# An attention block feeding a two-layer network: one attention stop on TensorE per chunk instead of two, and a new layout of the PSUM banks

## The chip, the cores and the metric

The kernel runs on one core of one Trainium2 chip. The metric is device microseconds of one execution, the median of several runs: 623.57 us for the kernel before (three runs, 623.25 to 624.53).

## The reference

Inputs are q, k and v of 4 batches, 8 heads, 768 positions and 64 features, and two weight matrices of 512 x 2048 and 2048 x 512. All numbers are float32. Each query sees the keys less than 16 positions away, and beside them 24 summary keys: the maximum over each block of 32 keys, whose values are the block's mean. The output of attention becomes 3072 rows of 512 numbers and goes through two layers with a squared ReLU between them.

```python
scores_l = scale * np.matmul(q, k.transpose(0, 1, 3, 2))
mask_l = np.abs(pos[:, None] - pos[None, :]) < window
scores_s = scale * np.einsum('bhsd,bhnd->bhsn', q, k_sum) + np.log(block)
a = np.exp(scores_all - np.max(scores_all, axis=-1, keepdims=True))
a = a / (np.sum(a, axis=-1, keepdims=True) + 1e-09)
attn = np.matmul(a, v_all)
h = np.maximum(x @ w_in, 0.0)
out = h * h @ w_out
```

## The kernel before

A *tile* is 128 positions of one batch with all 8 heads: 24 tiles, numbered 0 to 23, six to a batch. A *chunk* is two tiles, 256 rows of x: 12 chunks. The hidden width of 2048 is cut into 16 *f tiles* of 128.

**The two layers.** To keep float32 accuracy with the faster matmul format, x, the weights and the squares are each split in a high and a low part. `ffn1` (L380) does the first layer of one f tile for one chunk: 12 matmuls of 256 columns into half a PSUM bank. `squares` (L413) makes r = relu on ScalarE, the high part gh of r squared on ScalarE, the full square in PSUM on VectorE and the low part gl on VectorE. `ffn2` (L419) adds 6 matmuls of 512 columns for that f tile into the chunk's two output banks. When the 16th f tile is in, `evict` (L432) copies the outputs out of PSUM and stores them.

**The attention of a tile.** `scores_by_group` (L262) computes the scores of a tile: 32 small matmuls (64 in the trace, since a float32 matmul is two instructions) on array tiles of 64 x 32. `softmax` (L310) takes each head: VectorE scales, masks and takes the maximum (L300), ScalarE takes the exponential and its sum (L308). `inverse` and `norm` divide by the sum, norm on GpSimd. `turn` (L333) transposes the probabilities in 12 blocks on VectorE into pT. `outputs` (L348) multiplies them with the values: 16 matmuls (32 in the trace) on array tiles of 128 x 64 into the bank x_ps. `split_x` (L373) makes the high part xh on ScalarE and the low part xl on VectorE; these are the input of `ffn1`.

**The order of the work** is written out by hand, and each engine runs its part of it in that order. The first part, `START` (L43), is a list of tokens for tiles 0 to 5 and chunks 0 and 1 (F1 is ffn1, T is a transpose on TensorE, O outputs, S scores, PK place_k, KT and VT the reductions over key and value blocks, XH and XL the parts of split_x). The rest is a loop over chunks 2 to 11 in *slots* of two f tiles (L460): first layer of both, then second layer of the two f tiles before (`finish`), then the squares of this slot with the attention steps that belong to it, and at the end of the slot the steps in `last`, among them scores and outputs. `steps` (L474) gives each tile twelve steps, two to a slot; in chunk c the tiles 2c+2 to 2c+4 are at different steps (L622 to L624). So chunk c stops the two layers on TensorE twice: at the end of slot f = 2 for outputs of tile 2c+2 and scores of 2c+3, and at the end of slot f = 10 for outputs of 2c+3 and scores of 2c+4. Chunk 2 differs a little: there the scores of tile 7 and the outputs of tile 6 stand alone.

**PSUM** has eight banks: two for the scores of one tile (s_ps), one for x_ps, three that rotate for ffn1's results and for transposes (ph), two for the outputs (o_ps).

**Loads** go through SyncE's queue (SP): q, k and v of a tile two tiles ahead into buffers that two tiles share in turn, and for the next batch k and v transposed (kv) in four pieces, from which `sum_k` and `sum_v` (L174, L179) make the summary keys and values; `place_k` and `place_v` copy these beside a tile's own keys and values.

Of the kernel before, what the change touches and what calls it, by code (L numbers as in the profile page):

```python
# [73 lines left out]
def attn_ffn_kernel(ctx: ExitStack, tc: tile.TileContext, q, k, k0, kt, v, vt, v0, w, masks, gmasks, ident, mean, out):  # L74
# [7 lines left out]
    ps_x = ctx.enter_context(tc.tile_pool(name="ps_x", bufs=1, space=bass.MemoryType.PSUM))  # L82
    ps_h = ctx.enter_context(tc.tile_pool(name="ps_h", bufs=3, space=bass.MemoryType.PSUM))
# [26 lines left out]
    vsum = const.tile([P, NPAIR, 32], F32, name="vsum")  # L110

# [137 lines left out]
    def scores(g, p0, p1):  # L249


        if g not in s_ps:
            s_ps[g] = ps_s.tile([P, 2, NPAIR, P], F32, name="s_ps")
        for p in range(p0, p1):
            for r, s in ((0, 0), (1, 1), (0, 1), (1, 0)):
                rs, ss = slice(r * 64, r * 64 + 64), slice(s * 64, s * 64 + 64)
                nc.tensor.matmul(  # L257
                    s_ps[g][ss, r, p, 0:NK], lhsT=q_sb[g % 2][rs, s, p, :], rhs=by_run(g)[rs, :, s, p, :],
# [3 lines left out]
    def scores_by_group(g):  # L262

        s_ps[g] = ps_s.tile([P, 2, NPAIR, P], F32, name="s_ps")
        for p in range(NPAIR):
            for r, i in ((0, 0), (1, 2), (0, 1), (1, 3), (0, 2), (1, 0), (0, 3), (1, 1)):
                s, u = divmod(i, 2)  # L270
                rs = slice(r * 64, r * 64 + 64)
                nc.tensor.matmul(  # L272
                    s_ps[g][i * GQ : i * GQ + GQ, r, p, 0:GK], lhsT=q_sb[g % 2][rs, s, p, u * GQ : u * GQ + GQ],
                    rhs=by_pair(g)[rs, s, p, u * GQ : u * GQ + GK], start=True, stop=True,
                )

    def scores_kt(g, p0, p1):

        if g not in s_ps:
            s_ps[g] = ps_s.tile([P, 2, NPAIR, P], F32, name="s_ps")  # L280
        for p in range(p0, p1):
            for k0, k1 in ((0, 96), (96, NK)):
                for r, s in ((0, 0), (1, 1), (0, 1), (1, 0)):
# [4 lines left out]
                        s_ps[g][ss, r, p, k0:k1], lhsT=q_sb[g % 2][rs, s, p, :], rhs=keys, start=True, stop=True  # L288
                    )

    def mask_max(g, h):
# [5 lines left out]
        if half not in nmx:  # L297
# [3 lines left out]
            out=e_sb[:, h, 0:n], in0=s_ps[g][:, h % 2, h // 2, 0:n], in1=m, scale=-scale, scalar=3.0e38,  # L301
# [24 lines left out]
    def turn_pe(g, half):  # L326

        tp = ps_h.tile([P, 4, P], F32, name="ph")
# [19 lines left out]
    def outputs(g):  # L348
        x_ps[g] = xp = ps_x.tile([P, NPAIR, P], F32, name="x_ps")
# [30 lines left out]
    def ffn1(c, f):  # L380
        ph = ps_h.tile([P, 4, P], F32, name="ph").rearrange("p a b -> p (a b)")[:, 0:CT]
# [78 lines left out]
    def slot(c, f, side, last):  # L460
# [4 lines left out]
        for i in range(2):  # L465
            for do in side[i]:
                do()
# [3 lines left out]
        for do in last:  # L471
            do()
# [237 lines left out]
```

## Time and profile before

| | |
|---|---|
| median of three runs | 623.57 us (623.25 to 624.53) |
| the profiled execution | 624.3 us, its span 622.5 us |
| TensorE matmul busy | 597.6 us, 96% |
| VectorE busy | 404.8 us, 65% |
| ScalarE busy | 291.6 us, 47% |
| GpSimd busy | 89.7 us, 14% |
| mean granted TensorE clock | 0.992 |

PE is TensorE's matmuls, PEld its weight loads, DVE is VectorE, ACT is ScalarE, POOL is GpSimd and SP is SyncE, whose queue issues the transfers. A matmul's end is modelled and matmuls overlap, so a busy TensorE can still be slowed. A row of a group or of the timeline names the line of the kernel, the engine, the operation, the tile written and those read, the shape, and how many there are; in a timeline the first two numbers are start and length in us, and brackets tell how long the engine had been idle and what released it. The chain of waits follows the work that ended last, back from the end; its pieces also begin with start and length.

### The profile page before, as it was taken

The numbers are of one execution on the slowest core, as the hardware profiler recorded it, in microseconds if no ns is written. First come the engines' busy times: TensorE is split into PE (matmuls) and PEld (weight loads), VectorE is DVE, ScalarE is ACT, GpSimd is POOL, SyncE is SP. The second block draws the span as 40 slices with busy tenths as digits, with TensorE's granted clock in tenths as the row PEclk, the third lists the DMA queues.
The fourth block names the chain that finished last, engine by engine and source line by source line (L and its number), as shares of the span: only waits on it lengthen the run. The fifth ranks groups of instructions, "written<-read, shape, count | busy, mean of one in ns | idle before, by whom it ended". The sixth has DMA issues, their size and how long they took to land.

```text
span 622.5 us, 14548 instructions
## 1 busy us (share of the span) xinstructions
PE 597.6 (96%) x5792; PEld 535.7 (86%) x5792; DVE 404.8 (65%) x1237; ACT 291.6 (47%) x850; POOL 89.7 (14%) x83
## 2 busy tenths in 40 slices
PE   1699999999999999999999999999999999999997
PEld 1488888988989988998989989899889989889996
DVE  4889989767756757757558668566566566563222
ACT  2779887333444353443534444434525524433322
POOL 2555762001100000000100000001100000000000
PEclk9979999999999999999999999999999999999999
DMA  8999610464042341320331422411302300000000
GB/s 296 381 346 330 210 73 18 154 199 107 26 120 70 85 120 41 113 70 34 69 94 61 120 67 87 119 52 45 78 20 49 104 1 26 35 1 2 35 1 34
DMA packets 55107, 60.58 MB, mean 97 GB/s; under 512 B 40320, under 2 KB 40448, under 8 KB 52992
## 3 DMA queue, kind: packets, MB, share of 16 engines
q1 hardware_dynamic: 55040, 59.67, 31.7%
q8 instruction: 45, 0.74, 0.5%
q14 instruction: 22, 0.18, 0.1%
HBM read 53.36 MB, written 6.29 MB: 96 GB/s over the span
## 4 chain that ended last, share of the span: by engine, by line
PE 91%; DMA 3%; DVE 2%; ACT 2%; SPq 1%; issue 0%; POOL 0%; DVEq 0%; POOLq 0%
PE ph L385 42%; PE o_ps L426 41%; PE x_ps L354 4%; PE s_ps L272 2%; DMA w_raw<-in_w 2%; DMA q_sb<-in_q 2%; PE ph L330 1%; PE s_ps L287 0%; ACT e_sb L308 0%; DVE w_sb L243 0%; ACT w_sb L117 0%; PE s_ps L257 0%; SPq L167 0%; DVE sm L317 0%; SPq L121 0%
## 5 line engine op out<-in xcount | busy, mean ns | idle before, releaser
L385 PE MATMUL ph<-xh,w_sb 128*128 128x256 f32 x1536 | 272.5, 280 | 0.2 <-DVE gl L410 0.2
L385 PEld LDWEIGHTS ph<-xh,w_sb 128*128 128x128 f32 x1536 | 238.2, 189 | 9.2 <-DVE gl L410 0.4
L426 PE MATMUL o_ps<-w_sb,gh 128*128 128x512 f32 x768 | 238.0, 391 | 0.0
L385 PE MATMUL ph<-xl,w_sb 128*128 128x256 f32 x768 | 213.3, 278 | 0.3 <-DVE xl L371 0.3
L426 PEld LDWEIGHTS o_ps<-w_sb,gh 128*128 128x128 f32 x768 | 137.1, 188 | 24.9 <-issue 0.2
L426 PE MATMUL o_ps<-w_sb,gl 128*128 128x512 f32 x384 | 151.4, 394 | 0.9 <-DVE gl L410 0.9
L406 DVE TENSOR_TENSOR ph<-ph,r 128x256 f32<-128x256 f32 x192 | 82.5, 430 | 103.8 <-ACT r L394 101.4
L394 ACT ACTIVATE r<-ph 128x256 f32<-128x256 f32 x180 | 68.4, 380 | 170.9 <-PE ph L385 170.2
L385 PEld LDWEIGHTS ph<-xl,w_sb 128*128 128x128 f32 x768 | 144.9, 189 | 0.5 <-DVE xl L371 0.5
L308 ACT ACTIVATE e_sb<-e_sb,nmx 128x88 f32<-128x88 f32 (+1 forms) x192 | 70.1, 367 | 66.2 <-DVE nmx L300 66.2
L410 DVE TENSOR_TENSOR gl<-ph,gh 128x256 fp32r<-128x256 f32 x192 | 81.5, 425 | 23.7 <-PE ph L385 0.5
L341 DVE STREAM_TRANSPOSE pT<-e_sb 32x256 f32<-32x256 f32 x216 | 94.1, 436 | 3.4
L324 POOL TENSOR_TENSOR e_sb<-e_sb,sm 128x352 f32<-128x352 f32 (+1 forms) x43 | 35.8, 833 | 409.3 <-DVE nmx L300 355.2
L426 PEld LDWEIGHTS o_ps<-w_sb,gl 128*128 128x128 f32 x384 | 72.2, 188 | 15.7 <-DVE gl L410 1.3
L401 ACT ACTIVATE gh<-r 128x256 fp32r<-128x256 f32 x192 | 80.4, 419 | 11.4 <-DVE r L396 5.4
L371 DVE TENSOR_TENSOR xl<-x_ps,xh 128x512 fp32r<-128x512 f32 x24 | 16.6, 690 | 48.8 <-ACT xh L368 48.8
L368 ACT CAST xh<-x_ps 128x512 fp32r<-128x512 f32 x24 | 14.0, 583 | 54.0 <-PE x_ps L354 53.6
L236 POOL TENSOR_TENSOR w_raw<-w_raw 128x1024 int32<-128x1024 int32 x16 | 35.3, 2213 | 24.2 <-DVE w_raw L232 8.3
L354 PEld LDWEIGHTS x_ps<-pT,v_sb 128*64 128x64 f32 x768 | 25.4, 141 | 13.4 <-issue 11.4
L308 ACT ACTIVATION_READ_ACCUMULATOR e_sb<-e_sb,nmx 128x1 f32 x192 | 36.1, 188 | 0.0
L354 PE MATMUL x_ps<-pT,v_sb 128*64 128x64 f32 x768 | 29.0, 229 | 5.4 <-issue 4.1
L300 DVE CUSTOM_DVE_ANT_0 e_sb<-s_ps,gmask_sb 128x88 f32<-128x88 f32 x144 | 27.8, 240 | 0.1
(50 smaller groups left out, 297.3 us busy)
## 6 DMA issues: line engine op xcount, KB each, us to landing
w_raw<-in_w SPq DMA_DIRECT2D x16, 1024.0 KB, 14.1
v_sb<-in_v SPq DMA_DIRECT2D x24, 384.0 KB, 3.9
kv<-in_kt SPq DMA_DIRECT2D x16, 384.0 KB, 4.5
q_sb<-in_q SPq DMA_DIRECT2D x24, 256.0 KB, 4.6
out<-ob SPq DMA_DIRECT2D x24, 256.0 KB, 2.0
k_sb<-in_k SPq DMA_DIRECT2D x18, 256.0 KB, 5.0
kv<-in_vt SPq DMA_DIRECT2D x12, 384.0 KB, 3.8
k_sb<-in_k SPq DMA_DIRECT2D x18, 128.0 KB, 4.9
```

Of the source, the lines that this page charges most:

```text
L236: nc.gpsimd.tensor_tensor(out=hi, in0=hi, in1=lo, op=ALU.add)
L300: nc.vector.tensor_tensor_reduce(out=e_sb[:, h, 0:n], in0=s_ps[g][:, h % 2, h // 2, 0:n], in1=m, scale=-scale, scalar=3.0e38, op0=ALU.add, ...
L308: nc.scalar.activation(e, e, AF.Exp, bias=nmx[half][:, i : i + 1], scale=-1.0, accum_out=sm[half][:, i : i + 1])
L324: eng.tensor_mul(out=e, in0=e, in1=sm[half].unsqueeze(2).to_broadcast([P, 4, n]))
L341: nc.vector.transpose(out=pT[g % 2][j * 32 : j * 32 + 32, :, i * 32 : i * 32 + 32], in_=e_sb[i * 32 : i * 32 + 32, :, c : c + 32],)
L354: nc.tensor.matmul(xp[o : o + 64, h // 2, s * 64 : s * 64 + 64], lhsT=v_sb[g % 2][:, s, h * 64 : h * 64 + 64], rhs=pT[g % 2][:, h, s * 64 ...
L385: nc.tensor.matmul(ph, lhsT=w_sb[f][:, w, cc * P : (cc + 1) * P], rhs=x[c][:, cc, :], start=(n == 0), stop=(n == 3 * NC4 - 1))
L394: nc.scalar.activation(r, ph, AF.Relu)
L401: nc.scalar.activation(gh, r, AF.Square)
L406: nc.vector.tensor_mul(out=ph, in0=ph, in1=r)
L410: nc.vector.tensor_sub(out=gl, in0=ph, in1=gh.bitcast(F32))
L426: nc.tensor.matmul(o_ps[c][tt], lhsT=g_[:, ts_], rhs=w_sb[f][:, w, DM:], start=(first and n == 0), stop=(last and n == 2),)
```

## The change

Three things change together.

1. **The attention of a chunk is dealt anew.** `period(a)` replaces `steps(g)`: it holds the steps of tiles a and a+1 in eight slots, the first tile in the first four, the second in the last four. The two outputs stand together at the end of the eighth, and right behind them the scores of both next tiles, `scores_by_group` now doing two tiles at a time; then the four parts of split_x, and the loads of two tiles each. In chunk c the eighth slot of the period is f = 12. In the start, the scores of tile 7 come with those of tile 6, with the loads of its q and k and its place_k ahead of them.
2. **The banks are six fixed tiles.** Banks 0 and 1 take the scores of even tiles, 2 and 3 those of odd ones. Banks 4 and 5 are the first layer's, by turns from slot to slot, and take the outputs of an odd and an even tile. In the start, first-layer results and transposes take banks 3 to 5 from a list in order of release.
3. **Two f tiles share a bank,** one in each half, and `squares` works on both at once, 512 columns wide: one relu, one high square, one product, one difference where there were two of each.

```diff
@@ START, its end
-MU24 L:kw1 F1.25 GL24v L:v5 F1.26 RE25v MU25 SQ25 GL25v F2.23 XH4a RE26v MU26 XL4v F2.24 SQ26 GL26v KT1 F1.27
+MU24 L:kw1 F1.25 GL24v L:v5 L:k7 L:q7 F1.26 RE25v MU25 SQ25 GL25v F2.23 XH4a RE26v MU26 XL4v F2.24 SQ26 GL26v KT1 F1.27
-KT0 O5 PK6 VT0 S6.0 XH5a XL5v
+KT0 O5 PK6 VT0 PK7 XH5a S6.0 XL5v
@@ banks
-    ps_x = ctx.enter_context(tc.tile_pool(name="ps_x", bufs=1, space=bass.MemoryType.PSUM))
-    ps_h = ctx.enter_context(tc.tile_pool(name="ps_h", bufs=3, space=bass.MemoryType.PSUM))
+    r_sb = const.tile([P, 2, CT], F32, name="r")
+    gh_sb = const.tile([P, 4, CT], F32R, name="gh")
+    gl_sb = const.tile([P, 4, CT], F32R, name="gl")
+    bank = [ps_s.tile([P, DM], F32, name=n, tag=f"{n}{i}") for i, n in enumerate(["s_ps"] * 4 + ["ph"] * 2)]
@@ scores_by_group
+        for t in (g, g + 1):
+            s_ps[t] = [bank[t % 2 * 2 + r].rearrange("a (p k) -> a p k", p=NPAIR) for r in range(2)]
...
@@ outputs
-        x_ps[g] = xp = ps_x.tile([P, NPAIR, P], F32, name="x_ps")
+        xp = bank[2 if g < FROM_GROUPS - 1 else 5 if g < FROM_GROUPS else 5 - g % 2]
@@ squares
-    def squares(ph):
-        r = relu(ph, nc.scalar)
-        gh = high_square(r)
+    def squares(ph, k):
+        r = relu(ph, r_sb.rearrange("p a b -> p (a b)"), nc.scalar)
+        gh, gl = (b[:, 2 * k : 2 * k + 2, :].rearrange("p a b -> p (a b)") for b in (gh_sb, gl_sb))
+        high_square(gh, r)
         square(ph, r)
-        return gh, low_square(ph, gh)
+        low_square(gl, ph, gh)
+        return [(gh_sb[:, 2 * k + i, :], gl_sb[:, 2 * k + i, :]) for i in range(2)]
@@ slot
-        ph = [ffn1(c, f + i) for i in range(2)]
+        ph = bank[4 + f // 2 % 2]
+        for i in range(2):
+            ffn1(c, f + i, ph[:, i * CT : (i + 1) * CT])
         done = finish()
+        for do in before:
+            do()
+        for i, g_ in enumerate(squares(ph, f // 2 % 2)):
+            behind.append((c, f + i, *g_, f + i == 0, f + i == NF - 1))
...
+        for do in after:
+            do()
         for do in last:
             do()
@@ steps replaced by period
+    def period(a):
+        before, after, last = [[] for _ in range(8)], [[] for _ in range(8)], [[] for _ in range(8)]
+        b, t = divmod(a, NT)
+        if a >= n_g:
+            return before, after, last
+        if b and t == 0:
+            after[1] += [lambda: place_v(a), lambda: place_v(a + 1)]
+        after[0].append(lambda: softmax(a, 0, 3))
+        before[1].append(lambda: softmax(a, 3, 6))
+        after[1] += [lambda: softmax(a, 6, 8), lambda: inverse(0), lambda: norm(a, 0, nc.gpsimd)]
+        before[2] += [lambda: inverse(1), lambda: norm(a, 1, nc.gpsimd)]
+        after[2].append(lambda: turn(a, 0, 3))
+        before[3].append(lambda: turn(a, 3, 8))
+        after[3].append(lambda: turn(a, 8, 12))
+        before[4].append(lambda: softmax(a + 1, 0, 4))
+        after[4].append(lambda: softmax(a + 1, 4, 6))
+        before[5] += [lambda: softmax(a + 1, 6, 8), lambda: inverse(0), lambda: norm(a + 1, 0, nc.gpsimd)]
+        before[5] += [lambda: inverse(1), lambda: norm(a + 1, 1, nc.gpsimd)]
+        before[6].append(lambda: turn(a + 1, 0, 5))
+        after[6].append(lambda: turn(a + 1, 5, 8))
+        before[7].append(lambda: turn(a + 1, 8, 12))
+        if b + 1 < B and t:
+            for n, p in enumerate(((0, 1), (2, 3))[t // 4]):
+                last[3 * n].append(lambda p=p: load_kv(b + 1, p))
+                after[3 * n + 2].append(lambda p=p: sum_k(b + 1, p))
+                after[3 * n + 2].append(lambda p=p: sum_v(b + 1, p))
+        if b + 1 < B and t == 4:
+            after[6] += [lambda: place_k(a + 2), lambda: place_k(a + 3)]
+        last[7] += [lambda: outputs(a), lambda: outputs(a + 1)]
+        if a + 2 < n_g:
+            last[7].append(lambda: scores_by_group(a + 2))
+        last[7] += [lambda: split_x(a), lambda: split_x(a + 1)]
+        if a + 2 < n_g:
+            last[7] += [lambda g=g: load_v(g) for g in (a + 2, a + 3)]
+        if a + 4 < n_g:
+            last[7] += [lambda g=g: load_qk(g) for g in (a + 4, a + 5)]
+        return before, after, last
@@ the start's banks
+    free, held = [3, 4, 5], {}
...
         elif op == "F1":
-            ph_of[i] = ffn1(*units[i][:2])
+            held["F1", i] = free.pop(0)
+            ph_of[i] = ffn1(*units[i][:2], bank[held["F1", i]][:, 0:CT])
...
         elif op == "GL":
+            free.append(held.pop(("F1", i)))
@@ the loop
+        softmax(6, 0, 3)
...
             for f in range(0, NF, 2):
-                side, last = [[], []], []
-                at(side, last, 2 * c + 2, f + (4 if c == 2 else 6))
-                at(side, last, 2 * c + 3, f - 2)
-                at(side, last, 2 * c + 4, f - 10)
-                slot(c, f, side, last)
+                n = (f + 2) // 2 % 8
+                slot(c, f, *(w[n] for w in period(2 * c + (2 if n else 4))))
```

More of the change, by code (lines that the diff above doesn't have):

```diff
@@ L252, in scores @@
         if g not in s_ps:
-            s_ps[g] = ps_s.tile([P, 2, NPAIR, P], F32, name="s_ps")
+            s_ps[g] = [bank[r].rearrange("a (p k) -> a p k", p=NPAIR) for r in range(2)]
         for p in range(p0, p1):
@@ L389, in ffn1, with relu @@
         return ph
-    def relu(ph, eng):
-        r = work.tile([P, CT], F32, name="r", tag="r")
+    def relu(ph, r, eng):
         if eng is nc.scalar:
@@ L397, in relu, with high_square @@
         return r
[L399 to L400 removed]
+    def high_square(gh, r):
         nc.scalar.activation(gh, r, AF.Square)
```

92 lines of the change are left out of this document (26 added, 66 removed).

## The prediction

> **What bounds the kernel now.** I read the page first, then the chain of waits in order of time, then the timeline of TensorE around single attention blocks.
>
> ```profile
> span 622.5 us, 14548 instructions
> PE 597.6 (96%) x5792; PEld 535.7 (86%) x5792; DVE 404.8 (65%) x1237; ACT 291.6 (47%) x850; POOL 89.7 (14%) x83
> PE 91%; DMA 3%; DVE 2%; ACT 2%; SPq 1%; issue 0%; POOL 0%; DVEq 0%; POOLq 0%
> ```
>
> TensorE carries 91% of the chain. What matters is whether it ever waits after the written-out start. The chain shows one period of the steady part (start us, us, what):
>
> ```profile
> 198.07 1.08 PE x_ps L354 x32
> 199.15 0.89 PE s_ps L272 x60
> 200.04 2.94 PE ph L385 x24
> 202.98 2.75 PE o_ps L426 x12
> ...
> 208.47 2.75 PE o_ps L426 x12
> ...
> 213.96 2.75 PE o_ps L426 x12
> ...
> 219.46 2.75 PE o_ps L426 x12
> 222.21 1.08 PE x_ps L354 x32
> 223.29 0.89 PE s_ps L272 x60
> 224.17 1.91 PE ph L385 x15
> ```
>
> A plain slot (two f tiles) is 202.98 to 208.47, and three of them take 219.46 - 202.98 = 16.48, so 5.49 us each. From 200.04 to 224.17 are 24.13 us: four slots (21.97) and one attention block of one tile's outputs and another's scores, 2.16. There is no other engine in this chain, so a steady stretch costs exactly what TensorE's instructions and their changes of kind cost. Blocks with only outputs or only scores stand here:
>
> ```profile
> 141.22 2.80 PE o_ps L426 x12
> ...
> 146.76 2.75 PE o_ps L426 x12
> ...
> 153.42 2.76 PE o_ps L426 x12
> ...
> 160.20 2.75 PE o_ps L426 x12
> ```
>
> ```profile
> 557.32 2.75 PE o_ps L426 x12
> ...
> 564.09 2.75 PE o_ps L426 x12
> ```
>
> Less a slot of 5.49, scores of tile 7 alone cost 153.42 - 146.76 - 5.49 = 1.17, outputs of tile 6 alone 160.20 - 153.42 - 5.49 = 1.29, outputs of tile 23 alone 564.09 - 557.32 - 5.49 = 1.28.
>
> **What a block consists of.** The timeline of TensorE across one block:
>
> ```profile
> 197.68 0.40 PE L426 MATMUL o_ps<-w_sb,gl 128*128 128x512 f32 x1
> 198.00 1.15 PE L354 MATMUL x_ps<-pT,v_sb 128*64 128x64 f32 x32
> 199.08 0.96 PE L272 MATMUL s_ps<-k_sb,q_sb 64*32 64x88 f32 x64
> 199.97 0.50 PE L385 MATMUL ph<-xh,w_sb 128*128 128x256 f32 x2
> ```
>
> A 512-column matmul normally makes room for the next after 2.75/12 = 0.23 us, so outputs could begin at 197.91 and begin at 198.00: 0.09 lost. The 32 output instructions span 1.15 with their last one's own length; the form's mean is 0.22, so their starts span 0.93, while the scores begin only 1.08 after the first: 0.15 for the change of array shape where a pitch of 0.03 would do. The scores occupy 0.89 to the next first-layer matmul:
>
> ```profile
> 199.08:199.41 0.33, 0.33 (x32) 1.00 0.00 0
> 199.41:199.81 0.40, 0.40 (x56) 1.00 0.00 0
> ```
>
> These are two windows of the score matmuls alone: the first 32 begin within 0.33, the rest by 199.80, so 0.73 of starts and 0.16 of change back. The first-layer run then lasts 2.94 where others last 2.75. So of 2.16 about 0.93 + 0.74 are streaming and 0.49 are changes of kind.
>
> **The change, part by part.** Scores are issued for tiles 6 to 23, outputs likewise. Before: after scores of 6 in the start there are scores of 7 alone, outputs of 6 alone, 16 joint blocks, outputs of 23 alone. After: scores of 7 join those of 6, then 8 blocks of two outputs and two scores, then outputs of 22 and 23 together. Matmul counts, shapes and array tiles stay; only 10 of 19 interruptions go.
>
> *Second outputs in a block.* The trace has no two output sets in a row. Lower bound 0.93 (starts of one set), upper 1.08 (as before a change). I take 0.94: both sets use the same 128*64 tiles, so there is no change between them.
>
> *Second scores.* Lower bound twice the first half, 0.66; upper the whole block, 0.89. I take the middle, 0.77, since the second half above ran slower than the first. [...]
>
> *Sum in the steady part.* Before: 16 × 2.16 + 1.29 + 1.28 + 1.17 = 38.30. After: 8 × (2.16 + 0.94 + 0.77) = 30.96, and 1.28 + 0.94 = 2.22.
>
> *The end of the start.* The second place_k (PK7) now stands on VectorE ahead of the low half of x of tile 5, and scores of 7 stand on TensorE ahead of chunk 2:
>
> ```profile
> 136.38 0.26 DVE L187 COPY k_sb<-ksum 128x192 f32<-128x192 f32 x1
> 136.56 0.94 DVE L180 TENSOR_REDUCE vsum<-kv 128x24 f32<-128x768 f32 x1
> 136.72 0.96 PE L272 MATMUL s_ps<-k_sb,q_sb 64*32 64x88 f32 x64
> ...
> 137.53 0.18 DVE L183 TENSOR_SCALAR vsum<-vsum 128x24 f32<-128x24 f32 x1
> 137.61 0.50 PE L385 MATMUL ph<-xh,w_sb 128*128 128x256 f32 x2
> 137.62 0.68 DVE L371 TENSOR_TENSOR xl<-x_ps,xh 128x512 fp32r<-128x512 f32 x1
> ...
> 138.36 0.39 PE L385 MATMUL ph<-xl,w_sb 128*128 128x256 f32 x1 [0.25 <-DVE xl L371]
> ```
>
> Queued behind PK7 are only the low half and the softmax of 6. PK7 would run 137.62 to 137.88, scores of 7 from about 137.95, chunk 2 from 137.95 + 0.89 = 138.84; by then xl (0.25 later, at 138.55) is there. Before, chunk 2's first run began at 137.61 but its third matmul started only at 138.36. The whole stall shows in the chain above: the second-layer work begins at 141.22, where a first-layer run of 2.94 would have ended at 137.61 + 0.07 + 2.94 = 140.62 (the chain's pieces begin 0.07 after the timeline's, 200.04 against 199.97). So the old stall was 0.60, and the new cost is 138.84 - 137.61 - 0.60 = 0.63. Bounds: 0.25, where scores of 7 fit wholly into the stall and only PK7 shows, and 1.17, their price elsewhere. The loads of k and q for tile 7 move before the last kv load on SP; their buffers were free since the scores of 5, so nothing waits behind them.
>
> *Wide squares.* Per slot two relu, two squares, two products, two differences become one each of 512 columns. These rows price them:
>
> ```profile
> L406 DVE TENSOR_TENSOR ph<-ph,r 128x256 f32<-128x256 f32 x192 | 82.5, 430 | 103.8 <-ACT r L394 101.4
> L410 DVE TENSOR_TENSOR gl<-ph,gh 128x256 fp32r<-128x256 f32 x192 | 81.5, 425 | 23.7 <-PE ph L385 0.5
> L341 DVE STREAM_TRANSPOSE pT<-e_sb 32x256 f32<-32x256 f32 x216 | 94.1, 436 | 3.4
> L371 DVE TENSOR_TENSOR xl<-x_ps,xh 128x512 fp32r<-128x512 f32 x24 | 16.6, 690 | 48.8 <-ACT xh L368 48.8
> L368 ACT CAST xh<-x_ps 128x512 fp32r<-128x512 f32 x24 | 14.0, 583 | 54.0 <-PE x_ps L354 53.6
> ```
>
> A 512-wide operation takes 0.69 on VectorE and 0.58 on ScalarE, so a slot saves 2 × (0.43 + 0.425) - 2 × 0.69 = 0.33 on VectorE. It is worth nothing in the sum, since TensorE does not wait for it. It does make the chain longer: 0.58 + 2 × 0.69 and hand-overs, an estimated 2.4 us from the slot's last first-layer matmul, where the second-layer work of the slot before (2.75) and the next slot's first layer (2.75) cover 5.5. At the very end only 2.75 cover it, still enough; without cover it would cost at most 2.4 once.
>
> *New bank hand-overs.* Outputs of the even tile take bank 5, which the first layer of the next slot needs. This row belongs to the block shown above:
>
> ```profile
> 199.20 0.58 ACT L368 CAST xh<-x_ps 128x512 fp32r<-128x512 f32 x1 [3.01 <-PE x_ps L354]
> ```
>
> xh starts 0.27 after the last output matmul (198.00 + 0.93), so outputs to the end of xl take 0.93 + 0.27 + 0.58 + 0.69 and a hand-over, 2.5; the next first layer comes 1.08 + 0.94 + 0.77 + 0.89 = 3.68 after the outputs begin: 1.2 to spare. Outputs of the odd tile take bank 4, which the slot's own squares must leave: 2.4 against 2.75 + 1.08 = 3.8, 1.4 to spare. Both at nothing.
>
> *Total.* 38.30 - 30.96 - 2.22 - 0.63 = 4.5 us. The profiled execution took 624.3 (span 622.5 and 1.8 around it), so that run would be 619.8. It lies 0.7 above the median of the three runs, 623.57; against the median I forecast 619.1. Bounds of the unknown costs together: gain 38.30 - (8 × 4.13 + 2.36 + 1.17) = 1.7 at the least, 38.30 - (8 × 3.75 + 2.21 + 0.25) = 5.8 at the most, so 617.8 to 621.9.
>
> **The rivals.**
>
> *The blocks do not shrink.* If a second set pays as much as a set with its change (1.08 and 0.89), only entries and returns are saved and the gain is 1.7 to 2.3: 621.6. For it: no row shows two sets in a row. Against it: 0.15 and 0.16 lie plainly at the changes of shape, and within a set starts are 0.03 apart or less.
>
> *VectorE falls behind and TensorE waits: slower.* VectorE's work is dealt anew over the eight slots of a chunk. The heaviest are the one that turns the first three blocks (three transposes, the squares, and in two chunks of a batch both reductions with their scaling: 3 × 0.436 + 1.38 + 2 × 0.94 + 0.18 = 4.8) and the next (nine transposes and the squares, 3.9 + 1.4 = 5.3), of 5.49. The place where it decides is bank 5: the low half of x of the even tile stands in VectorE's queue behind four transposes and the squares, and the first layer waits for it. It turns the result when this low half is more than 1.2 + 4.5/8 = 1.8 us late in every chunk; at 2.5 us late the cost is 8 × 1.3 = 10.4, time 619.1 + 10.4 = 629.5. Against it: over a chunk VectorE needs 31 of 48 us (twice the 16.71 busy of one old period, the fourth column below, less 8 × 0.33), and lateness from the fourth slot has lighter slots behind it to run down in.
>
> ```profile
> 218.90:243.00 24.10, 24.10 (x242) 21.66 (x242) 16.71 (x54) 10.95 (x36) 1.55 (x2) 1.00 0.31 89
> ```
>
> *The start loses what the blocks gain.* Banks in the start come now from a list in order of release; five first-layer tiles and one transposed tile get another predecessor's bank than by rotation. If each came one VectorE operation later, it would be 6 × 0.43 = 2.6: 621.7. Against it: the list gives the bank that was released first, so most of them can only come earlier.
>
> **How the numbers follow.** Forecast 0.70; blocks that don't shrink 0.14; VectorE behind 0.07; the start loses 0.09. The measurement can't tell less than 0.2% (1.25 us) from no change, so faster means under 622.3: all of the forecast, most of the first and third rival (0.16 of 0.23), 0.86 with rounding; same 0.07; slower 0.07. The range 617.4 to 622.0 covers the bounds of the forecast and most of both mild rivals, and leaves out the slow one and a surplus below.
>
> **What would show it.** In the changed kernel's chain: 9 interruptions after the start where 19 were, quads of about 3.9 us (period 8 × 5.49 + 3.87 = 47.8), no other engine between them. The outputs' group should show 64 in a row with starts spanning 1.9, scores 128 in about 1.5. In the steady part TensorE should have no wait for xl, gl or pT; VectorE's busy time should fall by 10 × 8 × 0.33 = 26 us. It would be wrong if idle time of the first layer after xl appears once a chunk, or if a quad costs 4.3.

## The result, and the profile after

The changed kernel took 633.95 us (median of four runs, 631.23 to 634.45), the kernel before 623.43 in the same comparison: a ratio of 1.016, 95% interval 1.012 to 1.019. It is slower by 10.5 us. The forecast was 619.1 with a range of 617.4 to 622.0. The profiled execution took 633.53, its span 631.7 against 622.5 before, so 9.2 us are to be found. Three executions in the comparisons below took 858, 1198 and 2082 us, far above all others of their kernels, and no figure rests on them.

These are rows of the page of the changed kernel:

```profile
span 631.7 us, 14142 instructions
PE 601.6 (95%) x5792; PEld 545.1 (86%) x5792; DVE 385.4 (61%) x1077; ACT 262.5 (42%) x690; POOL 88.8 (14%) x83
PEclk9879999999999999999999998999999999999999
q8 instruction: 45, 0.74, 0.5%
PE 91%; DMA 4%; DVE 2%; issue 1%; SPq 1%; ACT 0%; DVEq 0%
```

VectorE and ScalarE have less to do, as meant (19.4 and 29.1 us less), and TensorE with the same 5792 matmuls is busy 4.0 us longer. "Issue", time in which an engine waits for nothing that the profile shows, was 0% of the chain and is 1%. The clock row has an 8 in the middle of the steady part. Queue q8 moved 45 instruction packets of some 16 KB, one for every 257 of TensorE's 11584 weight loads and matmuls. They keep step with TensorE's count (counted from 0, packet 14 began after 14.53 times 256 of them, packet 15 after 15.52, packet 18 after 18.56), so I read them as the supply of its instructions. A group of 256 is called a block below; the distances of the pauses in section 2 show that number.

**The blocks did shrink.** The chain of waits of the changed kernel around two quads (two outputs, two scores) that nothing disturbs:

```profile
226.66 2.72 PE o_ps L432 x12
...
232.99 3.02 PE ph L391 x24
236.01 2.72 PE o_ps L432 x12
238.73 2.83 PE ph L391 x24
...
260.92 2.83 PE ph L391 x24
...
274.84 2.72 PE o_ps L432 x12
277.55 2.02 PE ph L361 x64
279.57 1.59 PE s_ps L278 x113
281.16 2.93 PE ph L391 x24
284.09 0.92 PE o_ps L432 x4
```

Two outputs take 2.02, two scores 1.59. A plain slot is (260.92 - 238.73) / 4 = 5.55. The quads cost 236.01 - 226.66 - 5.55 = 3.80 and 284.09 - 274.84 - 5.55 = 3.70; 3.87 was forecast.

**The plain slot grew.** It was 5.49. The first layer's run of 24 matmuls is 2.83 instead of 2.75, the second layer's run of 12 is 2.72 instead of 2.75. Matmul by matmul, the first layer started every 113.3 ns before, after five starts at 116 to 122 behind each second-layer run; now it starts every 117.8 ns throughout. I call these the fast and the slow pitch. 71 of the slots have no block in them: 71 x 0.053 = 3.8 us.

**TensorE pauses in the quads.** The chain at the first and the fifth quad:

```profile
180.94 1.59 PE s_ps L278 x113
182.53 0.55 PE ph L391 x3
183.08 2.17 issue
```

```profile
378.31 2.62 issue
380.94 0.34 PE s_ps L278 x3
381.28 4.57 PE ph L391 x24
```

TensorE's waits for "issue" from 150 us to the end (us in total, times, longest), and two windows at the fifth quad (busy time of the engines, then granted clock, DMA share and GB/s):

```profile
PE s_ps L278 <- issue: 3.9, 3, 2.6
PE ph L391 <- issue: 2.2, 1, 2.2
```

```profile
377.50:381.80 4.30, 1.68 (x81) 1.36 (x69) 0.61 (x1) 0.00 (x0) 0.00 (x0) 1.00 1.02 259
381.80:385.30 3.50, 3.50 (x19) 3.50 (x18) 0.00 (x0) 0.00 (x0) 0.00 (x0) 0.51 0.92 204
```

No engine and no transfer of data releases these pauses. After the longest one the clock is granted at half for 3.5 us, which is why the following first-layer run takes 4.57. All TensorE starts of a quad and of the run behind it, less an undisturbed quad, give the table below. "Place" is how many TensorE instructions into a block of 256 the quad begins, counted over weight loads and matmuls.

```
quad begins  178.85  229.30  277.48  325.58  374.67  427.36  475.46  523.81
place            32     224     160      96      32     224     160      96
lost, us       2.35    0.09       0    0.98    4.55       0    0.22    0.85   sum 9.0
```

The place goes back by 64 from quad to quad, since a period has 960 instructions, and quads at 32 and 96 are the ones that lose. Before, no gap between two starts of TensorE in the steady part was above 0.33 us.

**Two smaller pieces.** The last block, outputs of 22 and 23 alone:

```profile
570.11 2.72 PE o_ps L432 x12
...
574.58 0.70 DVE xl L378
575.28 0.04 issue
575.32 3.09 PE ph L391 x24
578.41 2.72 PE o_ps L432 x12
```

It costs 578.41 - 570.11 - 5.55 = 2.75, not 2.22: with no scores behind the outputs, the next first layer waits for bank 5, which the even tile's low half has yet to leave. And the end of the start, in TensorE's timeline, first of the kernel before, then of the changed one:

```profile
135.54 1.25 PE L354 MATMUL x_ps<-pT,v_sb 128*64 128x64 f32 x32 [0.34 <-DVE pT L117]
...
137.61 0.50 PE L385 MATMUL ph<-xh,w_sb 128*128 128x256 f32 x2
```

```profile
136.63 1.25 PE L361 MATMUL ph<-pT,v_sb 128*64 128x64 f32 x32 [0.35 <-DVE pT L121]
137.80 0.96 PE L278 MATMUL s_ps<-k_sb,q_sb 64*32 64x88 f32 x64
139.02 0.96 PE L278 MATMUL s_ps<-k_sb,q_sb 64*32 64x88 f32 x64 [0.26 <-DVE k_sb L191]
139.90 0.51 PE L391 MATMUL ph<-xh,w_sb 128*128 128x256 f32 x2
```

From the outputs of tile 5 to chunk 2 it is 3.27 where it was 2.07; the old stall of 0.60 is gone, so 0.60 is lost, as forecast (0.63). The scores of tile 7 wait for its place_k, as forecast too. The outputs of tile 5 themselves come 1.1 us later than before.

**The sum.** Forecast was a span 4.5 shorter; it is 9.2 longer, 13.7 apart. Pauses 9.0, slow pitch 3.8, the start 1.1, the last block 0.5, less 8 x 0.07 to 0.17 for quads cheaper than forecast: 13.0 to 13.8.

### The profile page after: what moved, and what is told of

The parts are those of the page before. It is cut to its first block, busy times and chain, and to the rows that moved or that the text cites. A ratio compares the mean times of both kernels' runs of the same rounds, so it can differ in the third digit from the quotient of the medians.

```text
span 631.7 us, 14142 instructions
## 1 busy us (share of the span) xinstructions
PE 601.6 (95%) x5792; PEld 545.1 (86%) x5792; DVE 385.4 (61%) x1077; ACT 262.5 (42%) x690; POOL 88.8 (14%) x83
## 4 chain that ended last, share of the span: by engine, by line
PE 91%; DMA 4%; DVE 2%; issue 1%; SPq 1%; ACT 0%; DVEq 0%
PE ph L391 41%; PE o_ps L432 41%; DMA w_raw<-in_w 4%; PE ph L361 3%; PE s_ps L391 3%; PE s_ps L278 2%; DVE w_raw L236 1%; PE s_ps L361 1%; PE ph L336 0%; PE s_ps L293 0%; PE s_ps L261 0%; DVE w_sb L247 0%; SPq L171 0%; DVE sm L323 0%; ACT w_raw L225 0%
## 5 line engine op out<-in xcount | busy, mean ns | idle before, releaser
L391 PEld LDWEIGHTS ph<-xh,w_sb 128*128 128x128 f32 x1448 | 228.9, 190 | 10.7 <-issue 2.4
L391 PE MATMUL ph<-xl,w_sb 128*128 128x256 f32 x724 | 204.6, 283 | 0.0
L410 DVE TENSOR_TENSOR ph<-ph,r 128x512 f32<-128x512 f32 (+1 forms) x101 | 64.9, 643 | 160.5 <-ACT r L399 159.2
L399 ACT ACTIVATE r<-ph 128x512 f32<-128x512 f32 (+1 forms) x91 | 52.0, 571 | 226.0 <-PE ph L391 225.1
L413 DVE TENSOR_TENSOR gl<-ph,gh 128x512 fp32r<-128x512 f32 (+1 forms) x101 | 64.3, 637 | 10.5 <-DVE ph L410 0.5
L405 ACT ACTIVATE gh<-r 128x512 fp32r<-128x512 f32 (+1 forms) x112 | 64.0, 571 | 9.3 <-DVE r L401 5.8
L240 POOL TENSOR_TENSOR w_raw<-w_raw 128x1024 int32<-128x1024 int32 x16 | 35.6, 2233 | 25.4 <-DVE w_raw L236 8.7
L378 DVE TENSOR_TENSOR xl<-ph,xh 128x512 fp32r<-128x512 f32 x19 | 13.1, 691 | 22.4 <-ACT xh L375 22.4
L323 DVE TENSOR_SCALAR sm<-sm 128x4 f32<-128x4 f32 x48 | 13.4, 280 | 16.0 <-ACT e_sb L314 16.0
L375 ACT CAST xh<-ph 128x512 fp32r<-128x512 f32 x19 | 11.1, 587 | 26.6 <-PE ph L361 26.6
L361 PEld LDWEIGHTS ph<-pT,v_sb 128*64 128x64 f32 x608 | 18.6, 138 | 3.8 <-issue 3.2
```

The costliest lines, as they stand in the source:

```text
L240: nc.gpsimd.tensor_tensor(out=hi, in0=hi, in1=lo, op=ALU.add)
L361: nc.tensor.matmul(xp[o : o + 64, h // 2, s * 64 : s * 64 + 64], lhsT=v_sb[g % 2][:, s, h * 64 : h * 64 + 64], rhs=pT[g % 2][:, h, s * 64 ...
L391: nc.tensor.matmul(ph, lhsT=w_sb[f][:, w, cc * P : (cc + 1) * P], rhs=x[c][:, cc, :], start=(n == 0), stop=(n == 3 * NC4 - 1))
L399: nc.scalar.activation(r, ph, AF.Relu)
L405: nc.scalar.activation(gh, r, AF.Square)
L410: nc.vector.tensor_mul(out=ph, in0=ph, in1=r)
```

## The experiments

Medians of the kernel before beside them were 623.5 to 624.2. Ratios are to that kernel. Each kernel has one profile, of one of its runs; readings of pitch and pauses are of that run.

### 1. Where the tiles lie in SBUF

The change turned r, gh and gl from rotating work tiles behind xl into fixed tiles ahead of the weights, which moved the weights and x up by 10240 bytes a partition. Three kernels move tiles and nothing else. In the first, the changed kernel gets the old addresses (the two new pools are opened behind that of xh and xl):

```diff
-    r_sb = const.tile([P, 2, CT], F32, name="r")
-    gh_sb = const.tile([P, 4, CT], F32R, name="gh")
-    gl_sb = const.tile([P, 4, CT], F32R, name="gl")
+    late = ctx.enter_context(tc.tile_pool(name="late", bufs=1))
+    obs = ctx.enter_context(tc.tile_pool(name="obs", bufs=4))
+    r_sb = late.tile([P, 2, CT], F32, name="r")
+    gh_sb = late.tile([P, 4, CT], F32R, name="gh")
+    gl_sb = late.tile([P, 4, CT], F32R, name="gl")
```

> The changed kernel with r, gh and gl put back behind xh and xl, so that every SBUF tile (weights, xh, xl, r, gh, gl, ob) has the address that it had before; nothing else is edited. Theory A (the longer plain slot, 5.545 us against 5.49, comes from where the tiles lie in SBUF): ffn1's run of 24 matmuls falls from 2.83 to 2.75 us, the plain slot to 5.49, and with 80 plain slots and the 32 f tiles of the start the time falls by about 5.7 us, to 628 us. Theory B (it comes from the squares over two f tiles, or from two ph banks in turn instead of three): the run of 24 stays at 2.83, the slot at 5.545, the time at 634. Both: TensorE's pauses in and behind the quads stay at the first, fourth, fifth and eighth quad.

Measured: 626.65 us (625.13 to 631.85), ratio 1.005 (1.003 to 1.008): 7.3 us better than the changed kernel, where the pitch alone was to give 5.7; in its profile the quads also lose less. The run of 24 is 2.75 in seven of the eight chunks behind a full quad; in the one after the first quad it is 2.83 throughout. The pauses stay in the four quads (losses of 3.1, 1.2, 1.0 and 0.8 us, in all 6.1 instead of 9.0).

The second gives the kernel before the new addresses: `part` hands out the pieces of one fixed tile by turns, for r and gl as well:

```diff
-        gh = work.tile([P, CT], F32R, name="gh", tag="gh", bufs=4)
+        gh = part("gh", gh_sb, 4)
```

> The kernel before, with r, gh and gl held in fixed tiles that lie where the changed kernel has them, which moves the weights, xh and xl up by 10240 bytes a partition; squares of one f tile and the three ph banks stay. Theory A (addresses): the plain slot grows from 5.49 to about 5.545 us, ffn1's run of 24 from 2.75 to 2.83, the time from 623.4 to about 628 to 629 us. Theory B (squares or banks): slot 5.49, time 623.4.

Measured: 627.45 us (626.95 to 627.66), ratio 1.005 (1.004 to 1.007). Its chain in a stretch of plain slots:

```profile
206.20 2.83 PE ph L393 x24
209.03 2.72 PE o_ps L434 x12
```

That is the slot of the changed kernel, in all 60 of the first-layer runs that stand between two second-layer runs behind the start, without its banks, its squares or its quads. The rise is 3.2 instead of 4 to 5 us, as only 61 of its slots are plain: 61 x 0.053 = 3.2.

The third moves everything that TensorE reads in the two layers by the same 10240 bytes, keeping the distances (ob and r go ahead of the weights, an unused tile takes the place of r):

```diff
+    obs = [const.tile([P, DM], F32, name=f"ob{i}") for i in range(4)]
+    rs = [const.tile([P, CT], F32, name=f"r{i}") for i in range(2)]
...
+            pads.append(work.tile([P, DM], F32, name="pad", tag="pad", bufs=1))
```

> The kernel before, with ob and r in front of the weights instead of behind xl, so that the weights, xh, xl, gh and gl all move up by 10240 bytes a partition and keep the distances that they had to each other (the last kernel of this kind moved gh and gl below the weights as well, and had the slow pitch of 117.8 ns in all 48 runs of ffn1 after the blocks). Theory A1 (the distance of gh and gl to the weights and x decides): plain slots 5.49 us, time 623.5 to 624. Theory A2 (the place of the weights and x themselves decides): runs of 24 at 2.83 us, time 627 to 627.5.

Its chain in plain slots:

```profile
206.51 2.75 PE ph L387 x24
209.26 2.75 PE o_ps L433 x12
```

Measured: 624.96 us (622.34 to 625.70), ratio 1.000 (0.998 to 1.002), all plain runs fast. So weights and x 10240 bytes further up cost nothing by themselves, and the banks and the wide squares are not needed for the slow pitch: the place of gh and gl makes it. Whether that is their distance to the weights and x or their own address is not told apart: 10240 is five times 2048, so an effect that repeated every 2048 bytes, say, would look the same here. Nor is it shown how the place comes to matter, since the first layer's matmuls read x and weights, and neither gh nor gl.

### 2. Where a quad begins in a block of instructions

Two kernels put 64 empty instructions per period on TensorE's queue, to make a period 1024 instructions long.

```diff
         done = finish()
+        if c > 2 and f in (2, 4, 6, 8):
+            for _ in range(16):
+                nc.tensor.nop(nofuse=True)
```

> The changed kernel with 64 empty instructions on TensorE's queue in each period (16 in each of four plain slots, where the queue is far ahead of the matmuls) and 160 at the end of the start. They make a period 1024 instructions long, four fetched blocks of 256, so that every quad begins at the same place of a block, 192. Theory F (the pauses are late fetches of TensorE's own instructions, and come only where a quad begins some 32 to 96 instructions into a block): no pause over 0.3 us in any quad, each 3.6 us long; the time falls by about 9 us, to 625. Rival G (the pauses come from banks, semaphores or the loads that share the moment): the same quads pause (178, 325, 374, 523 us), time 634.

> The same empty instructions, 64 in each period, but none at the end of the start: every quad begins 32 instructions into a block, as the first and fifth do in the changed kernel, which paused for 2.3 and 4.5 us. Theory F (late instruction fetches): all eight quads pause, for 2.3 to 3 us each or more, 18 to 24 us in all instead of 9; the time rises by 9 to 15 us, to 643 to 649 us. Rival G: the same four quads pause, time 634; if the empty instructions themselves cost, this kernel and the one with the place 192 rise alike.

Measured: 635.03 and 633.14 us, and nothing learned on the places: both profiles have 45 packets on q8 as before, so the empty instructions were not in the programs that ran. They are two more runs of the changed kernel, and all three profiles pause at the same four instructions, numbers 3495, 6302, 7323 and 10130, which is 13.65, 24.62, 28.61 and 39.57 times 256. The pauses belong to places in the program.

Real instructions did it. Cutting a second-layer matmul of 512 columns in two adds a weight load and a matmul. `halved` is true for odd f from the first quad on, 32 cuts a period, and in the first kernel also for 20 f tiles of the start. Both have the old addresses:

```diff
+                cut = g_ is gh and halved(c, f)
+                for h in range(2 if cut else 1):
+                    hs = slice(h * CT, (h + 1) * CT) if cut else slice(0, DM)
                     nc.tensor.matmul(
-                        o_ps[c][tt], lhsT=g_[:, ts_], rhs=w_sb[f][:, w, DM:],
+                        o_ps[c][tt][:, hs], lhsT=g_[:, ts_], rhs=w_sb[f][:, w, DM:][:, hs],
```

> On the kernel with the old addresses (626.65 us). ffn2's matmuls of 512 columns with the gh weights are cut into two of 256 columns on the same bank: in 20 f tiles of the start and in 8 f tiles of each period, 32 more pairs of weight load and matmul a period, so that a period has 1024 instructions of TensorE and every quad begins 192 instructions into a block of 256 (the empty instructions of the last try were not in the program that ran: 45 blocks fetched, as before). 226.7 ns for 512 columns and 113.3 for 256 say that the cut itself costs about nothing, at most 8 ns a pair. Theory F (the pauses are late fetches, and the place where a quad begins in a block decides): no pause over 0.33 us in any of the eight quads; the 6.8 us of pauses of that kernel's profile go, time about 619.5 to 621. Rival G (banks, semaphores): the same quads pause, time 626.5.

> The same cuts in each period, none in the start: every quad begins 32 instructions into a block. Theory F: all eight quads pause, by 1 to 3 us each; with some 16 to 24 us of pauses instead of 6.8 the time goes to 636 to 644. Rival G: as in the kernel without cuts, 626.5.

Measured: 626.59 us (623.61 to 631.56) with all quads at 192, 651.72 (649.08 and 654.37) with all at 32, more than the 636 to 644 expected: behind three of its pauses the clock was at half for 3.4 us, and two chunks ran at the slow pitch. What each quad lost:

```
all at 192   0.15  0.18  0     0.09  0.06  0.14  0.02  0.01   sum 0.7
all at 32    2.26  4.18  2.63  1.24  3.25  4.52  4.55  1.32   sum 24.0
```

Waits of TensorE with all at 32, from 150 to 630 us:

```profile
PE s_ps L280 <- issue: 10.3, 5, 2.9
PE ph L393 <- issue: 7.2, 3, 2.7
```

The two differ in their cuts in the start and in where the blocks' borders then fall. Theory F holds for the pauses: the place decides. (The dense run at the end of the start, 320 instructions long, fell on place 120 in the first kernel and paused for 0.96.)

Why the pauses stand at 0.57 to 0.66 of a block shows when the semaphore instructions of TensorE's queue are counted too, three with each quad. Then all 29 pauses of 0.4 us or more in seven profiles (the changed kernel, the one with the old addresses, the two with empty instructions, these two and the one of section 3) stop at the same place of a block of 256, 193 instructions into it by this count. In the changed kernel they stand 2816, 1024 and 2816 instructions apart, which is 11, 4 and 11 times 256. And each ends 1.2 to 1.7 us after the end of a transfer on q8 (in the changed kernel 1.44, 1.61, 1.47 and 1.33). I read this so: TensorE stands at the border of a block and goes on once the next one has come.

The forecast of the time for the first kernel failed by 6 us: its profiled run, the quickest of ten, still has two chunks of eight at the slow pitch, and the others were not profiled.

### 3. Loads out of the way

In the changed kernel the loads of q, k and v are issued in the quad. The queues' packets in two windows of the first quad, up to the pause and within it:

```profile
q1 hardware_dynamic: 90, 0.36, 39.0%
```

```profile
q1 hardware_dynamic: 435, 0.71, 92.2%
q8 instruction: 1, 0.02, 2.2%
```

No instruction packet came in 178.85 to 182.30; one came in 182.30 to 185.30, while data filled 92% of the DMA engines. Counted in blocks of 256 that TensorE has worked through, transfer number k (the first is number 0) begins at about k + 0.5 in plain slots, some 1.1 blocks ahead of the next place of a pause (k + 1.57 to 1.65). Number 12 began at 13.64, and TensorE stood still at 13.65. Do the loads make it late, or does TensorE's queue? On the old addresses, without cuts:

```diff
+    def hold():
+        nc.sync.dma_start(out=mark, in_=gh_sb[0:1, 0, 0:1].bitcast(F32))
...
-            last[7] += [lambda g=g: load_v(g) for g in (a + 2, a + 3)]
+            last[1].append(hold)
+            last[1] += [lambda g=g: load_v(g) for g in (a, a + 1)]
```

> On the kernel with the old addresses, no cuts. The loads of q, k and v that were issued in the quad (8 transfers, 1 MB) are held back by two slots: one transfer of 4 bytes that waits for a gh tile of the slot after next stands ahead of them in SP's queue. The quads begin where they did (32, 224, 160, 96 instructions into a block). Theory F2 (the fetch of instructions is late because these loads fill the same DMA engines in the quad): no pause over 0.33 us, time about 619 to 620. Theory F1 (TensorE's sequencer itself does not ask for the next block, or not in time, while it issues some 380 instructions in 3.6 us): the pauses of 1 to 2.5 us stay in the same quads, time 626 to 627.

Measured: 623.85 us (622.77 to 626.20), ratio 1.000 (0.999 to 1.002), 2.8 us better than with the loads in the quad. From 150 to 630 us TensorE waits for "issue":

```profile
PE s_ps L281 <- issue: 2.4, 3, 1.2
PE ph L394 <- issue: 0.9, 1, 0.9
```

The same four quads pause, for 1.1, 1.15, 1.55 and 0.6, in all 4.4 us with nothing else on the DMA engines (their share in the first quad is 0.02). Transfer number 12 now begins at 13.29, not at 13.64, and TensorE still stands at 13.65. So both theories have a share: the loads delay the fetch, and without them it is still too late. A quad's 384 instructions go by in 3.6 us, 9.4 ns each, where a plain slot's 72 take 5.5 us, 76 ns each; 256 instructions last 19 us in plain slots and 2.4 in a quad, and a packet on q8 takes 0.88 to 1.45 in the profile of the changed kernel. The attention blocks of the kernel before have 192 instructions, fewer than a block of 256, and no gap between two starts in them was above 0.33.

### 4. No pauses at all, and the pitch again

Late loads and every quad at place 164, by 66 cuts in chunk 2 and 32 in each period:

```diff
+    def halved(c, f, g_, gh):
+        return (f % 2 == 1 and g_ is gh) if 16 * c + f > 43 else c == 2 and 0 < f < 12
```

> Old addresses, loads held back by two slots, and the cuts of ffn2's matmuls: 66 in chunk 2 before the first quad (132 instructions), 32 in each period after it, so that every quad begins 164 instructions into a block; nothing is cut in the start. Theory F (late fetches, made later by the loads): no pause over 0.4 us in the eight quads, where the kernel with late loads alone (623.85 us) had 4.3 us of them in its profile; time 619 to 620.5. Rival (what is left of the pauses is not the place in a block): 623.5 to 624, with pauses in the first, fourth, fifth and eighth quad.

Measured: 624.87 us (623.43 to 629.02), ratio 1.003 (1.001 to 1.005). From 150 to 630 us TensorE has one wait left, that of the last block:

```profile
PE ph L394 <- DVE xl L381: 0.5, 1, 0.5
```

The pauses are gone from every full quad, as theory F says, and yet the time did not fall: three of the eight stretches behind full quads ran at the slow pitch, a period of 48.9 us instead of 47.7, and chunk 2 changed between both (the expectations below count it as the fourth). With the cuts the slow pitch costs more, 2.83 and 2.80 against 2.73 and 2.76 for the two runs of a slot. Behind these quads a chunk took one pitch and kept it. Then the same cuts put together ahead of the quad:

```diff
-        return (f % 2 == 1 and g_ is gh) if 16 * c + f > 43 else c == 2 and 0 < f < 12
+        return 0 < f < 12 if c == 2 else c > 2 and (7 <= f <= 11 or (f == 6 and g_ is gh and w == 0))
```

> As the kernel with late loads and every quad 164 instructions into a block (624.87 us, no pause in any quad, but four of its eight chunks ran ffn1 at the slow pitch, 2.83 instead of 2.73 us a run, 1.2 us a chunk), with the 32 cuts of a period put together in the three slots ahead of the quad (f tiles 6 to 11) instead of in every slot. Theory P (the cut in every slot is what lets a chunk stay at the slow pitch): all chunks at 2.75 or less, no pauses, time 619 to 620.5. Theory Q (a chunk takes its pitch by how it leaves the quad, whatever stands in its slots): some chunks slow again, time 621 to 625.

Measured: 623.99 us (621.96 to 625.48), ratio 1.000 (0.999 to 1.002); no pause, three chunks slow, and one of the cut slots of each other chunk too. Theory P falls.

Last, gh and gl moved up by 320, 832 and 1856 bytes in the kernel with quads at 164:

```diff
+    late.tile([P, 320 // 4], F32, name="gap")
     gh_sb = late.tile([P, 4, CT], F32R, name="gh")
```

> The kernel without pauses (every quad 164 instructions into a block, late loads, 624.87 us, four of eight chunks at the slow pitch) with gh and gl, and ob behind them, 320 bytes a partition further up, nothing else moved: the distance of gh to a weight tile goes from 2240 to 2560 modulo 8192 (0 in the changed kernel, which was slow in all chunks). Theory A (the distance of gh and gl to the weights sets the pitch): the number of slow chunks changes; with none 619 to 620.5, with all 629. Theory Q (where they may be fast, a chunk's pitch falls out as it leaves the quad, and the distance plays no part): three to five slow chunks, 623 to 626.

> The same with 832 bytes: the distance of gh to a weight tile is 3072 modulo 8192, a multiple of 1024 as 0 and 4096 are. Theory A in the form that a multiple of 1024 or 2048 is what makes the pitch slow: all chunks slow, 628 to 630; in the form that only 0 modulo 8192 is bad: fewer slow chunks, 619 to 622. Theory Q: three to five slow chunks, 623 to 626.

> The same with 1856 bytes: gh lies 4096 and gl 0 modulo 8192 from a weight tile, as gl and gh do in the changed kernel. Theory A (the distance decides): all chunks slow as there, 628 to 630. Theory Q: three to five slow chunks, 623 to 626.

Measured: 628.61, 627.79 and 628.72 us, ratios 1.007, 1.007 and 1.007 (each 1.004 to 1.009). No pauses, and in every chunk the pitch changes from slot to slot. The times come near what theory A gave for chunks slow throughout, but by luck, as the traces show something else. The chain with 1856 bytes:

```profile
285.76 2.83 PE ph L395 x24
288.59 2.80 PE o_ps L442 x16
291.38 2.75 PE ph L395 x24
```

Slots use the two pairs of gh and gl tiles by turns. So the place of gh and gl (ob moved with them) does change the pitch, against theory Q; but three distances did the same, and no simple rule of the distance in theory A foresaw slow and fast by turns. Which places are good, and why single chunks go slow at the old ones, stays open.

### 5. The wide squares

The kernel with late loads and old addresses, with squares over one f tile each in the new banks:

```diff
-        r = relu(ph, r_sb.rearrange("p a b -> p (a b)"), nc.scalar)
...
+        for i in range(2):
+            half = ph[:, i * CT : (i + 1) * CT]
+            r, gh, gl = r_sb[:, i, :], gh_sb[:, 2 * k + i, :], gl_sb[:, 2 * k + i, :]
+            relu(half, r, nc.scalar)
+            high_square(gh, r)
+            square(half, r)
+            low_square(gl, half, gh)
```

> The kernel with late loads and old addresses, with relu, high square, square and low square over one f tile again (256 columns, eight operations a slot instead of four), the banks as they are. Theory of the prediction (the wide squares are worth nothing, they lie beside TensorE): 623.9 us, within 0.5. Rival (the shorter chain of wide squares is part of what the change brings, or the banks are now handed over too late): VectorE and ScalarE need about 0.3 us more a slot, ffn1 waits for its bank, slower by 2 us or more.

> The kernel with squares over one f tile once more, for its profile. It took 638 to 642 us against 623.85 with wide squares: 16 us, 0.2 us a slot. Theory T (the chain behind ffn1 is too long: the four operations of the second f tile stand behind those of the first, so gl comes after the 2.75 us of the next ffn2 cover): ffn2 waits for gl, or ffn1 for its bank, by about 0.2 us in each slot, 14 to 17 us in all. Rival (a slow pitch or more pauses of TensorE): no waits for VectorE over 2 us in all, ffn1's runs of 24 at 2.83 us, and pauses in the quads.

Measured: 639.27 us the first time (three runs, 638.48 to 642.24), 637.34 the second (635.74 and 638.94), ratio 1.022 (1.019 to 1.025). Against wide squares that is 15.4 and 13.5 us. TensorE's waits, from the profile of the second:

```profile
PE ph L364 <- DVE gl L416: 10.7, 4, 2.9
```

and VectorE's timeline ahead of the second quad, the first of the four:

```profile
223.88 3.14 DVE L350 STREAM_TRANSPOSE pT<-e_sb 32x256 f32<-32x256 f32 x7
...
229.01 0.42 DVE L416 TENSOR_TENSOR gl<-ph,gh 128x256 fp32r<-128x256 f32 x1
```

The second outputs go to the bank that this slot's squares must leave. VectorE comes to them behind a row of transposes and is done at 229.43, while the first outputs ended near 226.9; in four of eight quads 2.7 to 3.1 us pass between two starts of TensorE, three times followed by the clock at half for 3.4 us. Both theories are off: it is a wait for VectorE, but four long ones and not 0.2 in each slot.

## Why the prediction was wrong

- **The steady part costs what TensorE's instructions cost, plain slot 5.49.** This step failed. I carried the slot over as a constant. It depends on where gh and gl lie in SBUF, which the diff changes: 5.55, 3.8 us over 71 slots. That was shown by moving tiles alone, both ways (sections 1 and 4); by what mechanism stays open.
- **Quad of 3.87 us.** Its parts were right or too high: second outputs 0.94 forecast, 2.02 - 1.08 = 0.94 measured; second scores 0.77 forecast, 1.59 - 0.89 = 0.70 measured. With no pauses the quad is 3.7 to 3.8, and the rival in which blocks don't shrink falls.
- **The quad priced as a pitch times a count.** This step failed, and it is the largest. 384 instructions in 3.6 us overtake the supply of instructions: 9.0 us of pauses with what they do to the clock. No rival had this mechanism. The supply is the same before and after, 45 packets on q8 for 11584 instructions; in the steady part of the kernel before it held TensorE up nowhere, as no gap was above 0.33 us, and here it did, for up to 2.86 us between two starts.
- **The end of the start, 0.63.** Right, 0.60. The start itself lost another 1.1 before that, the size of half the third rival. Kernels of the series spread by over 2 us from their first matmul to the outputs of tile 5 (127.7 to 130.4) without regard to the pitch, so its cause stays open.
- **Bank hand-overs at nothing.** Right for full quads: no wait for xl or gl there. Wrong for the last block, where the scores that give the 1.2 us to spare are missing: 0.5.
- **Wide squares at nothing.** The sum of the step stands, as TensorE did not wait for the squares behind the start of the changed kernel. The reading of it was wrong: I looked for what they save and found it hidden, and they are what keeps the slow rival away. With narrow squares (old addresses, late loads) VectorE falls behind at bank 4, as that rival had it at bank 5, for 13.5 us or more.
- **VectorE 26 us less busy.** Right for the operations meant. The squares took 82.5 + 81.5 = 164.0 us of VectorE before, by the rows of the prediction. After, these rows of the page hold most of them, the 160 wide ones among them at 0.69 to 0.70 each:

```profile
L410 DVE TENSOR_TENSOR ph<-ph,r 128x512 f32<-128x512 f32 (+1 forms) x101 | 64.9, 643 | 160.5 <-ACT r L399 159.2
L413 DVE TENSOR_TENSOR gl<-ph,gh 128x512 fp32r<-128x512 f32 (+1 forms) x101 | 64.3, 637 | 10.5 <-DVE ph L410 0.5
```

With 9.4 for those of the start in another bank that is 138.6, so 25.4 less. The page's busy time fell by 19.4 only, as it counts once what overlaps; the other operations on VectorE hardly changed (276.7 and 277.0 by the sums of their groups).
- **The signs of being wrong.** Neither of the two named came: there is no wait for xl once a chunk, and undisturbed quads cost 3.7 to 3.8, not 4.3. Both looked at the banks and at the blocks' parts, and the loss came from the supply of instructions and from the place of tiles.

With the old addresses and late loads the change is worth nothing either way (ratio 1.000); take away its profile's 4.4 us of pauses and that run (623.07) would stand at 618.7, near the forecast of 619.1, by arithmetic only. No kernel run here has both no pauses and the fast pitch throughout, and none beats the kernel before beyond its interval.

## What to carry to other kernels

When small instructions are put together, count them: here quads of 384 TensorE instructions at 9.4 ns each outran the supply of instructions, which the joint blocks of 192 did not, and what that cost hung on where in a block of 256 the quads began (0.7 to 24.0 us) and on what else was on the DMA queues (6.1 us lost with the loads in the quad, 4.4 us of pauses with them later, at the same addresses). A new layout of tiles is a change of its own, so time it alone, with every other edit left out. And an edit that shortens an idle engine's work may still be what holds a new order together: price it without the others.

## What the runs showed of the hardware that was not expected

- TensorE paused for 0.4 to 3.1 us in dense runs, 29 times in seven profiles, always 193 instructions into a block of 256, and went on 1.2 to 1.7 us after the end of an instruction transfer on q8. Moving the quads against the blocks by added instructions took the loss to 0.7 us or to 24.0, from 6.1 with the same addresses.
- Of 17 pauses and waits of 2.3 to 3.1 us between two starts of TensorE, 12 were followed by the clock at half for 3.4 us, and none of those up to 1.5 us was. Length alone does not decide: one of 2.30 was followed by it, one of 3.09 was not. In the changed kernel it cost another 1.5 us once.
- The first layer ran at two pitches, 113.3 and 117.8 ns a matmul, with the same instructions. Where no second-layer matmul was cut, a chunk kept its pitch from one quad to the next. With gh and gl ahead of the weights all slots were slow (2.83 in 60 of 60 runs), with them 320, 832 or 1856 bytes above their old place every other slot (2.83 and 2.75 by turns), and at the old place single chunks or none. Where all slots are slow the second layer's run of 12 is a little faster, 2.72 against 2.75; in a single slow chunk it is slower, 2.77.
- 64 outputs and 128 scores in a row took 15.7 ns a TensorE instruction for outputs (2.02 us) and 6.2 for scores (1.59), where 32 and 64 in a row took 16.9 (1.08) and 6.9 (0.89) before.
